# Pooling attention and a residual MLP on one core: the first batch recorded in parts by a written list, token weights in two transfers

## The chip, the cores and the metric

One core of a Trainium2 chip. The metric is the device time of one execution in microseconds (us). The kernel has five compute engines: TensorE (PE) for matmuls and transposes, VectorE (DVE), ScalarE (ACT), GpSimd (POOL), and SyncE (SP), which here only issues transfers. Transfers are also issued by POOL (all those that change the number format on the way) and a few by ACT.

## The reference

Eight batches, eight heads, 576 positions, head width 64. Keys and values are averaged over groups of eight positions, so that each query sees 72 of them; the attention output, heads side by side, is the input x of a residual MLP of width 512.

```python
k_p = k.reshape(B, H, Sp, pool, D).mean(axis=3)
v_p = v.reshape(B, H, Sp, pool, D).mean(axis=3)
scores = scale * np.matmul(q, k_p.transpose(0, 1, 3, 2))
scores = scores - np.max(scores, axis=-1, keepdims=True)
attn = np.exp(scores)
attn = attn / (np.sum(attn, axis=-1, keepdims=True) + 1e-09)
x = np.matmul(attn, v_p)        # heads then side by side: (8, 576, 512)

a1 = alpha1 * x + beta1
tok = np.einsum('ts,bsd->btd', w_tok, a1)
u = x + lam * tok
a2 = alpha2 * u + beta2
ch = np.maximum(a2 @ w_ch1, 0.0) @ w_ch2
out = u + lam * ch
```

## The kernel before

Positions are handled in chunks of 128: four whole chunks per batch, and the last 64 positions of two batches together as a fifth. Four chunks make a block of 512 tokens for the MLP; there are nine. Work is recorded in a fixed order and each engine runs its own instructions in that order, one after another; waits between engines go over semaphores. From the second batch on, the order comes from a list of due times per block (the loop over `n` near the end): while the MLP of one block runs, the attention of the next batch is strewn in. The first batch has no MLP to hide under. Its order, from `load_w1(0)` to the last `mlp_A(0, j, 256, 512)`, is written out by hand, and this opening is what is changed.

The parts of the opening, with their lines in the kernel before:

- Loads. q, k, v of batch 0, the token weights (`load_wtok`, L387 for the four main rows per partition and L391 for the last 64 rows), the first part of w_ch1 (`load_w1(0)`, L560), then q (L267) and k (L281) of batch 1 are all issued by POOL, ahead of its own arithmetic. The other parts of w_ch1, v of batch 1 and w_ch2 (`load_w1`, `load_v32`, `load_w2`) are issued by POOL further on, between its other work.
- Attention of batch 0. `att_F` transposes q for two heads on PE (L594) and copies it out of PSUM; `att_Frem` does so for the last 64 positions. `double_k` and `cast_rem_k` prepare k on DVE; `att_K` averages k with matmuls (L671, L677); `first_V` does the same for v (L698, L700). `att_S` is the scores of one head in two halves (L719, L722), each followed by its exponential on ACT (L724). `att_AV` multiplies by v (L783, L787); DVE takes the reciprocal of the sum and scales (L789, L791).
- Input of the token product. `spread_lamal` spreads lambda times alpha1 over all partitions with a matmul (L503) and a copy. `att_X` multiplies two heads of x by it into `xs` (L805), `rest_X` does so for the last positions (L798); in the opening most of these run on POOL. `bias_row` writes the beta1 row of `xs` on DVE (L478).
- Token weights. `setup_wtok` transposes 128 rows of the token weights on PE (L521) and ACT copies them to `wtT` (L524). `setup_rowsum` sums the columns with matmuls (L533) and ACT copies one row (L535). `setup_vectors` turns beta2 and alpha2 into columns (L508 to L512).
- Token product and first layer. `mix_T` multiplies a chunk's `wtT` by `xs` (L869, five matmuls of 512 columns), DVE adds x (L873), and DVE or POOL multiplies by alpha2 (L879). `mix_uT` transposes the result (L893), ACT copies it to `u_fm` (L895). `mlp_A` is the first MLP layer (L917): in block 0 the hidden parts 0 to 3 are done for the first 256 tokens and then for the second 256, with the bias column taken on DVE (L920) and the ReLU on ACT (L924).

PSUM has eight banks. Six belong to the pool `psA`, from which `gp` hands out one bank after another in turn; two belong to `psB`, which the opening before uses only for the warm-up matmuls (`keep_warm`, L860). A new tile in a bank waits until the last reader of the old one is done.

Before the change a part is a function that records its matmuls and the copy out of PSUM at once, so that a later part's matmul comes behind the earlier part's copy in the list, though on another engine:

```python
setup_wtok(0, nc.scalar.copy)
att_AV(0, 6)
load_rem(1, behind=nc.vector)
setup_wtok(1, nc.scalar.copy)
```

Of the kernel before, what the change touches and what calls it, by code (L numbers as in the profile page):

```python
# [210 lines left out]
def kernel(  # L211
# [27 lines left out]

    def gp(name):  # L240
        return psA.tile([P, 512], FP, tag="gp", name=name)

# [256 lines left out]
    def spread_lamal(half, copy):  # L499

        ps = gp("ps_bc")[:, 0:256]
        cols = slice(256 * half, 256 * half + 256)
        nc.tensor.matmul(out=ps, lhsT=ones_row, rhs=vecs[0:1, 2, cols])  # L503
        copy(out=lamal_bc[:, cols], in_=ps)

    def setup_vectors():
        ps = gp("ps_vec")
        nc.tensor.transpose(out=ps[:, 0:8], in_=b2row, identity=identity[0:8, 0:8])  # L508
        nc.scalar.copy(out=b2c_bf, in_=ps[:, 0:4])
        nc.scalar.copy(out=al2_cols, in_=ps[:, 4:8])  # L510
        u_fm[0] = work.tile([P, 4, 2, 258], BF, tag="u_fm", bufs=3, name="u_fm")
        nc.scalar.copy(out=u_fm[0][:, :, 0, 256], in_=ps[:, 0:4])  # L512

    def setup_wtok(tcx, copy):

        trc = P if tcx < 4 else REM
        w = wt_bf[0:trc, S * tcx:S * tcx + 640]
        strided = w[:, 0:512].rearrange("p (m c) -> p c m", c=4)
        ps_w = gp("ps_w").bitcast(BF)
        for sc in range(5):  # L520
            nc.tensor.transpose(out=ps_w[0:P, trc * sc:trc * sc + trc],  # L521
                                in_=strided[:, sc, :] if sc < 4 else w[:, 512:640],
                                identity=identity_bf[0:trc, 0:trc])
        copy(out=wtT[:, 0:5, P * tcx:P * tcx + trc],  # L524
             in_=ps_w[:, 0:5 * trc].rearrange("p (s t) -> p s t", t=trc))

    def setup_rowsum(tcx):

        trc = P if tcx < 4 else REM
        cols = slice(P * tcx, P * tcx + trc)  # L530
        ps = gp("ps_rs")
        for sc in range(5):
            nc.tensor.matmul(out=ps[:, 0:trc], lhsT=ones_bf if sc < 4 else ones_lo,  # L533
                             rhs=wtT[:, sc, cols], start=(sc == 0), stop=(sc == 4))
        nc.scalar.copy(out=wtT[64:65, 4, cols], in_=ps[64:65, 0:trc])  # L535
# [44 lines left out]
    def att_F(b, hp, copy=nc.scalar.copy):  # L580
# [4 lines left out]
        if r == 0:  # L585
# [14 lines left out]
        def finish(copy):  # L600
            copy(out=st["qT"][u][:, 4 * r:4 * r + 4, :],
                 in_=ps_q[:, 0:512].rearrange("p (c t) -> p c t", c=4))

        if copy is None:
            return finish
        finish(copy)

    def att_Frem(b, copy=None):
# [14 lines left out]
        for c in range(2):  # L623
            nc.tensor.transpose(out=ps_q[:, 128 * c:128 * c + 128],
                                in_=st["rem"][0][:, c].rearrange("p h d -> p (h d)"),
                                identity=identity_bf)
        copy(out=st["rem_qT"], in_=ps_q[:, 0:256].rearrange("p (c t) -> p c t", c=2))

    def double_k(u):

        nc.vector.tensor_copy(out=st1[0]["k"][u][:, :, 4], in_=st1[0]["k"][u][:, :, 0])
        if u == 0:
            cast_rem_k(nc.vector)
# [29 lines left out]
    def att_K(b, u, copy):  # L663
# [18 lines left out]
        if b:  # L682
            copy(out=kp_pool[u], in_=kp)
            return
        for a in range(2):
            rows = slice(64 * a, 64 * a + 64)
            (copy or (nc.scalar.copy, nc.vector.tensor_copy)[a])(
                out=kpT_pool[u][rows, a], in_=kp[rows])

    def first_V(b, u, copy=nc.vector.tensor_copy):  # L690
# [8 lines left out]
        for c in range(nr):  # L699
            nc.tensor.matmul(out=vp, lhsT=pool_vr if b else pool_vr[0:32],  # L700
                             rhs=rest[:, heads, c], start=False,
                             stop=(c == nr - 1))
        copy(out=vp1_pool[u][:, :, 0:64], in_=vp.rearrange("p (h d) -> p h d", h=4))
# [8 lines left out]
    def att_S(b, h):  # L712
        st = st1[b]
        u, r, hh = h // 4, h // 2 % 2, h % 2
        ET = ET_pool[u][:, h % 4]
        for half in range(2):
            n0, n = 256 * half, 256 + 64 * half
            ps_sc = gp("ps_sc")
            nc.tensor.matmul(out=ps_sc[0:SPG, 0:256], lhsT=kpT_pool[u][:, half, h % 4, :],  # L719
                             rhs=st["qT"][u][:, 2 * (h % 4):2 * (h % 4) + 2, :])  # L720
            if half:
                nc.tensor.matmul(out=ps_sc[0:SPG, 256:320], lhsT=kpT_pool[u][:, hh, h % 4, :],  # L722
                                 rhs=st["rem_qT"][:, :, h // 2::4].rearrange("p c i -> p i c"))
            nc.scalar.activation(out=ET[:, n0:n0 + n], in_=ps_sc[0:SPG, 0:n],  # L724
                                 func=AF.Exp, bias=0.0, scale=0.125)
# [47 lines left out]
    def att_AV(b, h):  # L773
# [13 lines left out]
        nc.tensor.matmul(out=av[:, 4 - 4 * odd, :], lhsT=ET[:, r0:r0 + 128], rhs=vp1[:, h % 4, :])  # L787
        rec = recs[:, h, b, :]
# [53 lines left out]
    u_fm = {}  # L842
# [19 lines left out]
    def mix_T(b, c, eng=nc.vector):  # L862
# [3 lines left out]
        for sc in range(5):  # L866
            for i, p0, p1 in parts:
                kk, at = (P, sc) if sc < 4 else (P, 5) if i else (65, 4)
                nc.tensor.matmul(out=ps_tok[p0:p1], lhsT=wtT[0:kk, at, P * c:P * c + p1 - p0],  # L869
                                 rhs=xs_pool[i][0:kk, sc, :], start=(sc == 0), stop=(sc == 4))  # L870
        for i, p0, p1 in parts:
# [3 lines left out]
                                    in1=ps_tok[p0:p1, 0:DM], op=ALU.add)  # L875
        if b:
# [4 lines left out]
    def mix_uT(key):  # L881
# [10 lines left out]
        for cc in range(4):  # L892
            nc.tensor.transpose(out=ps_uT[0:P, 128 * cc:128 * cc + 128],  # L893
                                in_=s["u_bf"][:, 128 * cc:128 * cc + 128], identity=identity_bf)
        nc.scalar.copy(out=u_fm[blk][:, :, at // 2, 128 * (at % 2):128 * (at % 2) + 128],  # L895
# [10 lines left out]
    def mlp_A(n, j, t0=0, t1=512):  # L906
# [5 lines left out]
        for cc in range(4):  # L912
            if n == 0:
                rhs = u_fm[0][:, cc, 0, 0:257] if one else u_fm[0][:, cc, t0 // 256:2, 0:256]
            else:
                rhs = u_fm[n][:, cc, :]
            nc.tensor.matmul(out=ps_h[:, t0:t1 + one], lhsT=w1_of(cc, j), rhs=rhs,  # L917
                             start=(cc == 0), stop=(cc == 3))
        if one:
# [138 lines left out]
    for u in range(2):  # L1058
        load_k(1, u, queue=nc.gpsimd)
    keep_warm(16)  # L1060
    att_F(0, 0)
    second_copy = att_F(0, 1, None)
    cast_rem(0, nc.vector)
    more_constants()
    rem_copy = []
    att_Frem(0, lambda **io: rem_copy.append(io))
    double_k(0)
    second_copy(nc.vector.tensor_copy)
    att_K(0, 0, None)
    nc.scalar.copy(**rem_copy[0])  # L1070
    first_V(0, 0)
    bias_row(0)
    att_S(0, 0)
    att_S(0, 1)
    double_k(1)
    att_S(0, 2)
    att_AV(0, 0)
    spread_lamal(0, nc.vector.tensor_copy)
    att_AV(0, 1)
    att_S(0, 3)  # L1080
    att_K(0, 1, nc.scalar.copy)
    att_F(0, 2, nc.vector.tensor_copy)
    att_AV(0, 2)
    late_copy = att_F(0, 3, None)
    att_X(0, 0, 2, nc.gpsimd, False)
    spread_lamal(1, nc.scalar.copy)
    att_S(0, 4)
    late_copy(nc.scalar.copy)
    att_AV(0, 3)
    att_X(0, 2, 4, nc.gpsimd, False)  # L1090
    first_V(0, 1)
    att_S(0, 5)
    load_al2(nc.vector)
    att_AV(0, 4)
    att_S(0, 6)
    rest_X(0, 0, 4, nc.gpsimd)
    att_AV(0, 5)
    att_X(0, 4, 6, nc.gpsimd, False)
    att_S(0, 7)
    setup_wtok(0, nc.scalar.copy)  # L1100
    att_AV(0, 6)
    load_rem(1, behind=nc.vector)
    setup_wtok(1, nc.scalar.copy)
    att_AV(0, 7)
    setup_rowsum(0)
    setup_wtok(2, nc.scalar.copy)
    rest_X(0, 4, 6, nc.gpsimd)
    load_w1(1)
    setup_wtok(3, nc.scalar.copy)
    setup_rowsum(1)  # L1110
    setup_vectors()
    setup_wtok(4, nc.scalar.copy)
    att_X(0, 6, 8)
    bias_row(1)
    mix_T(0, 0, nc.gpsimd)
    setup_rowsum(2)
    load_w1(2)
    mix_T(0, 1)
    setup_rowsum(3)
    load_lam(nc.vector)  # L1120
    mix_T(0, 2, nc.gpsimd)
    load_v32(1)
    mix_uT((0, 0))
    mix_uT((0, 1))
    mix_T(0, 3)
    load_w2(0)
    load_w2(1)
    mlp_A(0, 0, 0, 256)
    mix_uT((0, 2))
    mlp_A(0, 1, 0, 256)  # L1130
    mlp_A(0, 2, 0, 256)
    mix_uT((0, 3))
    mlp_A(0, 3, 0, 256)
    for j in range(4):
        mlp_A(0, j, 256, 512)


    def attention(b):
# [4 lines left out]
        if first:  # L1143
            for hp in range(4):
                todo.append((2.6 + 0.9 * hp, lambda hp=hp: att_F(b, hp)))
# [3 lines left out]
            todo.append((7.4, lambda: att_Frem(b, nc.scalar.copy)))  # L1149
        if b < B - 1:  # L1150
            at = 28.5 if first else 10.0
            todo.append((at, lambda: att_F(b + 1, 0)))
            todo.append((at + 0.1, lambda: att_F(b + 1, 2)))
            todo.append((19.3 if first else 23.1, lambda: cast_rem(
                b + 1, nc.gpsimd, behind=None if first else nc.vector)))
            todo.append((26.72 if b > 1 else 26.22, lambda: att_Frem(b + 1)))
        for u in range(2):
# [8 lines left out]
            if first:  # L1166
                todo.append((19.1 + 0.1 * u, lambda u=u: sum_k(2, u, nc.gpsimd)))
            todo.append((7.0 + 2.3 * u if first else 2.9 + 2.0 * u,
                         lambda u=u: att_K(b, u, nc.vector.tensor_copy if first else nc.scalar.copy)))
        for u in range(2):  # L1170
# [5 lines left out]
            for i, dt in enumerate((2.9, 3.4, 4.6, 5.1) if u else early):  # L1176
                h = 4 * u + i
                todo.append((at + dt, lambda h=h: att_AV(b, h)))
# [3 lines left out]
        if first:  # L1182
            for i, u in enumerate((0, 2, 1)):
                todo.append((10.6 + 0.1 * i, lambda u=u: sum_v(b, u)))
            for u in range(2):
                todo.append((12.3 + 1.0 * u, lambda u=u: first_V(b, u)))
# [3 lines left out]
        for c in range(5):  # L1190
            at = 22.0 + 1.1 * c if first else 21.0 + (1.3 if b == 2 else 1.15) * c
            if c < 4 or b % 2:
                todo.append((at, lambda c=c: mix_T(b, c)))
                key = (b, c) if c < 4 else (b - 1, 4)
                todo.append((at + 1.8, lambda key=key: mix_uT(key)))
        return todo

    for n in range(NBLK):
        todo = []
        for j in range(0 if n else 4, NJ):  # L1200
            if n == 0 and j < 8:
                todo.append((j, lambda j=j: mlp_A(0, j, 0, 256)))
                todo.append((j + (1.01 if j < 7 else 0.3), lambda j=j: mlp_A(0, j, 256, 512)))
            else:
                at = 8 * (j // 4 % 2) + 4 * (j // 8) + j % 4 if n >= FIRST else j
                todo.append((at, lambda j=j: mlp_A(n, j)))
# [51 lines left out]
        if n == 0:  # L1258
            todo.append((6.2, lambda: setup_rowsum(4)))
# [58 lines left out]
```

## Time and profile before

| | |
|---|---|
| Median of 3 runs | 331.59 us (330.57 to 332.87) |
| Profiled execution | 331.99 us, of which the span is 330.5 us |
| PE busy | 320.9 us (97%) |
| DVE busy | 235.0 us (71%) |
| ACT busy | 174.5 us (53%) |
| POOL busy | 117.8 us (36%) |
| Moved by transfers | 47.72 MB, 144 GB/s over the span |

The span is the time from the first to the last instruction that the profile shows; the profiled execution's own time is 1.5 us longer. Shares are over the whole span and hide that stages have different limits. A row of the timeline gives start, duration, engine, line, operation, what is written from what, how many instructions of the kind follow each other, and in brackets the idle time ahead of it with what ended it. Where several matmuls are in one row, the duration runs to the end of the last one, which is pipelined, so that the start of the next row tells better how long they kept PE. For a transfer, the duration of the instruction is only the issue; its landing is given apart.

### The profile page before, as it was taken

The page shows a single profiled execution, that of the slowest core. Times are in us where ns is not written, and L with a number is a line of the kernel's source. Part 1 is how long each engine was busy: PE and PEld are TensorE (multiplying, and loading weights), DVE is VectorE, ACT ScalarE, POOL GpSimd, SP SyncE. Part 2 cuts the span into 40 slices and gives each one's busy share as a digit, 9 for nine tenths or more (in the row PEclk, how much of TensorE's full clock was granted, in tenths as well). Part 3 has the DMA queues.
Part 4 walks back from the last instruction along what each step waited for, and adds up shares of the span by engine and source line. Part 5 has one row for each costly group of instructions (what it writes and reads, how often), then busy time and mean ns, then how long its engine had stood idle before and what let it go on. Part 6 is the DMA issues. An engine that isn't in the chain of part 4 may idle for free.

```text
span 330.5 us, 6433 instructions
## 1 busy us (share of the span) xinstructions
PE 320.9 (97%) x2436; PEld 206.6 (63%) x2467; DVE 235.0 (71%) x495; ACT 174.5 (53%) x323; POOL 117.8 (36%) x142
## 2 busy tenths in 40 slices
PE   8989999999999999999999999999999999999995
PEld 3657764445544567656775676558755866586584
DVE  6764276897769979787869787877788793263263
ACT  1675989459522871288028812682268225703710
POOL 8859625997238001800271026202520560000000
PEclk9999999999999999999999999999999999999999
DMA  7999999957897993399439953998560025003013
GB/s 105 191 219 293 277 180 234 182 134 186 167 258 107 194 178 126 82 242 195 156 80 216 214 161 77 173 202 154 144 170 9 2 51 160 0 2 127 0 34 95
DMA packets 73370, 47.72 MB, mean 144 GB/s; under 512 B 41165, under 2 KB 63829, under 8 KB 73338
## 3 DMA queue, kind: packets, MB, share of 16 engines
q1 hardware_dynamic: 58876, 34.50, 44.8%
q0 software_dynamic: 13856, 12.40, 22.4%
q10 hardware_dynamic: 606, 0.40, 0.5%
q8 instruction: 19, 0.31, 0.4%
q14 instruction: 13, 0.11, 0.1%
HBM read 38.57 MB, written 9.44 MB: 145 GB/s over the span
## 4 chain that ended last, share of the span: by engine, by line
PE 89%; DMA 3%; DVE 3%; POOL 2%; issue 1%; ACT 0%; POOLq 0%
PE ps_h L917 38%; PE ps_w L1033 26%; PE ps_tok L869 11%; PE ps_ch L937 7%; DMA wt_bf<-in_moe_w_tok_dram 3%; PE ps_s L739 2%; PE ps_av L783 2%; DVE w L968 1%; DVE u_sb L873 1%; PE ps_r L746 1%; PE ps_av L787 1%; POOL v L301 0%; POOL k L273 0%; ACT wtT L524 0%; POOL u_bf L879 0%
## 5 line engine op out<-in xcount | busy, mean ns | idle before, releaser
L917 PE MATMUL ps_h<-u_fm,w 128*128 128x512 bf16 (+2 forms) x588 | 131.3, 368 | 1.7 <-DVE u_sb L947 0.6
L924 ACT ACTIVATE H<-ps_h,bias_cols 128x512 bf16<-128x512 f32 x144 | 98.1, 688 | 55.4 <-PE ps_h L917 54.0
L917 PEld LDWEIGHTS <-w 128*128 128x128 bf16 x608 | 65.9, 114 | 51.4 <-issue 3.3
L1033 PEld LDWEIGHTS <-H 128*128 128x128 bf16 x560 | 53.5, 98 | 10.8 <-DVE u_sb L1051 1.2
L877 ACT CAST u_bf<-u_sb 128x512 bf16<-128x512 f32 x32 | 19.8, 618 | 70.7 <-issue 41.8
L1033 PE MATMUL ps_w<-w,H 128*128 128x256 bf16 x448 | 53.6, 273 | 0.0
L805 POOL TENSOR_TENSOR xs<-x_tm,lamal_bc 128x512 bf16<-128x512 f32 x12 | 15.2, 1268 | 105.0 <-DVE x_tm L791 104.5
L1051 DVE TENSOR_TENSOR u_sb<-u_sb,ps_w 128x512 f32<-128x512 f32 x54 | 36.4, 684 | 17.9 <-PE ps_w L1033 17.0
L869 PE MATMUL ps_tok<-xs,wtT 128*128 128x512 bf16 (+2 forms) x193 | 44.5, 380 | 0.7 <-DVE xs L805 0.3
L873 DVE TENSOR_TENSOR u_sb<-x_tm,ps_tok 128x512 f32<-128x512 f32 (+1 forms) x40 | 27.4, 684 | 9.8 <-PE ps_tok L869 9.8
L791 DVE TENSOR_TENSOR x_tm<-ps_av,recs 128x320 f32<-128x320 f32 x64 | 31.5, 491 | 2.7
L768 ACT ACTIVATE ET<-ps_s 72x512 f16<-72x512 f32 x56 | 32.3, 592 | 0.0
L937 PE MATMUL ps_ch<-w,H 128*128 128x512 bf16 x124 | 30.0, 379 | 0.2
L869 PEld LDWEIGHTS <-wtT 128*128 128x128 bf16 (+3 forms) x200 | 17.4, 100 | 16.4 <-issue 1.1
L789 DVE RECIPROCAL recs<-ps_av 128x5 f32<-128x5 f32 x64 | 12.1, 189 | 19.0 <-PE ps_av L787 18.8
L709 DVE TENSOR_TENSOR v_u<-v_u 72x1024 f32<-72x1024 f32 (+1 forms) x24 | 23.6, 985 | 0.2
L1033 PE MATMUL ps_w<-w_t,h_s 128*128 128x256 bf16 x168 | 22.6, 272 | 0.0
L937 PEld LDWEIGHTS <-H 128*128 128x128 bf16 x128 | 11.9, 98 | 13.7 <-issue 0.4
L378 POOL TENSOR_TENSOR k_raw<-k_raw 128x512 f32<-128x512 f32 x14 | 19.1, 1367 | 3.5 <-DMA k_raw<-in_k_dram 3.5
L380 POOL TENSOR_TENSOR k_bf<-k_raw 128x512 bf16<-128x512 f32 x14 | 19.2, 1370 | 1.1
L1002 DVE TENSOR_TENSOR h_s<-H 128x1024 bf16<-128x1024 bf16 x21 | 14.6, 696 | 6.3 <-ACT H L924 5.8
L1033 PEld LDWEIGHTS <-h_s 128*128 128x128 bf16 x168 | 16.4, 98 | 4.1
(165 smaller groups left out, 358.1 us busy)
## 6 DMA issues: line engine op xcount, KB each, us to landing
out_dram<-u_sb SPq DMA_DIRECT2D x29, 256.0 KB, 4.3
k_raw<-in_k_dram SPq DMA_DIRECT2D x12, 512.0 KB, 6.0
v_u<-in_v_dram SPq DMA_DIRECT2D x12, 512.0 KB
q_bf<-in_q_dram POOLq DMA_DIRECT2D x16, 256.0 KB, 6.1
w<-in_moe_w_ch_dram POOLq DMA_DIRECT2D x6, 512.0 KB, 13.3
out_dram<-u_sb SPq DMA_DIRECT2D x11, 128.0 KB, 2.2
w<-in_moe_w_ch_dram POOLq DMA_DIRECT2D x1, 1024.0 KB, 14.5
k_raw<-in_k_dram POOLq DMA_DIRECT2D x2, 512.0 KB, 16.8
```

Source lines behind the costliest of these rows:

```text
L380: eng.tensor_tensor(out=bf, in0=twice[0], in1=twice[1], op=ALU.add)
L709: nc.vector.tensor_tensor(out=out, in0=t[:, :, 0:width], in1=t[:, :, width:2 * width], op=ALU.add)
L768: nc.scalar.activation(out=o, in_=i, func=AF.Exp, bias=0.0, scale=0.125 if b < 3 else 0.125 * 0.125)
L791: nc.vector.tensor_tensor(out=x[:, 1 - odd:6 - odd, dd:dd + D], in0=av[:, :, 0:64], in1=rec.unsqueeze(2).to_broadcast((P, 5, D)), op=ALU.mult)
L869: nc.tensor.matmul(out=ps_tok[p0:p1], lhsT=wtT[0:kk, at, P * c:P * c + p1 - p0], rhs=xs_pool[i][0:kk, sc, :], start=(sc == 0), stop=(sc == 4))
L873: nc.vector.tensor_tensor(out=s["u"][p0:p1, :], in0=x[p0:p1, 1 + c if c < 4 else 5 - 5 * i, :], in1=ps_tok[p0:p1, 0:DM], op=ALU.add)
L877: nc.scalar.copy(out=s["u_bf"], in_=s["u"])
L917: nc.tensor.matmul(out=ps_h[:, t0:t1 + one], lhsT=w1_of(cc, j), rhs=rhs, start=(cc == 0), stop=(cc == 3))
L924: nc.scalar.activation(out=H4[n, j // 4][:, j % 4, :], in_=ps_h, func=AF.Relu, bias=bias_cols[:, j:j + 1], scale=1.0)
L937: nc.tensor.matmul(out=ps, lhsT=H_of(n, j)[:, 128 * m:128 * m + 128], rhs=w2[j // 4][:, j % 4, :], start=(j == 0), stop=(j == NJ - 1))
L1033: nc.tensor.matmul(out=ps, lhsT=stat(j), rhs=moving(j), stop=(j == 7), start=(first and (pp == 0 or alone) and j == 0), skip_group_check=True)
L1051: nc.vector.tensor_tensor(out=o, in0=o, in1=banks[key, "both"], op=ALU.add)
```

## The change

The opening is recorded in parts. The functions become generators: the matmuls of a part are recorded up to a `yield`, the copy or the arithmetic on the result at the next call. A dictionary `plan` holds one generator under a short name for each part, and a written list of names, `order`, says which of them is taken one step further. For the rest of the kernel `whole` runs a generator to its end at once, which records the same as before.

With it come these edits:

- `load_wtok` issues the four main rows in two transfers of 1216 and 1088 columns instead of one of 2304. The first serves W0 and W1, the second W2 and (with the short transfer) W3.
- `spread_lamal` (s0, s1) stands ahead of k on PE.
- Seventeen of the opening's PSUM tiles, named in `in_pair`, come from `psB` instead of `psA`, so that eight banks turn instead of six.
- The heads are done in another order (2, 3, 1, 0, 5, 4, 7, 6 or near to it, halves apart), some copies change their engine, and the `xs` pieces (X and R) change their order.
- The k loads of batch 1 (k0, k1) go from ahead of the opening to between the parts; the second and third part of w_ch1 (l1, l2) go ahead of k0 and k1. v of batch 1 (lv) and two parts of w_ch2 (l3, l4) stand between the token products.

In the names, F, K, V, S, A, X, R, W, r, M, T, H and G stand for `att_F`, `att_K`, `first_V`, the scores, `att_AV`, `att_X`, `rest_X`, `setup_wtok`, `setup_rowsum`, `mix_T`, `mix_uT`, and the two halves of `mlp_A`.

```diff
+    pair = [False]
+
     def gp(name):
+        if pair[0]:
+            return psB.tile([P, 512], FP, tag="ch", bufs=2, name=name)
         return psA.tile([P, 512], FP, tag="gp", name=name)
+
+    def whole(parts):
+        for _ in parts:
+            pass
...
     def load_wtok():
-        nc.gpsimd.dma_start(out=wt_bf[:, 0:4 * S],
-                            in_=moe_w_tok[0:512, :].rearrange("(p c) s -> p (c s)", c=4))
+        main = moe_w_tok[0:512, :].rearrange("(p c) s -> p (c s)", c=4)
+        for c0, c1 in ((0, 2 * S + 64), (2 * S + 64, 4 * S)):
+            nc.gpsimd.dma_start(out=wt_bf[:, c0:c1], in_=main[:, c0:c1])
...
         nc.tensor.matmul(out=ps, lhsT=ones_row, rhs=vecs[0:1, 2, cols])
+        yield
         copy(out=lamal_bc[:, cols], in_=ps)
...
     load_q_bf(1, 0)
     load_q_bf(1, 1)
-    for u in range(2):
-        load_k(1, u, queue=nc.gpsimd)
     keep_warm(16)
...
+    plan = {"dr": once(lambda: cast_rem_k(nc.vector)), "b0": once(lambda: bias_row(0)),
+            "b1": once(lambda: bias_row(1)), "Fr": att_Frem(0, vector),
+            "ve": setup_vectors(), "la": once(lambda: load_al2(nc.vector)),
+            "lr": once(lambda: load_rem(1, behind=nc.vector)),
+            "ll": once(lambda: load_lam(nc.vector)), "lv": once(lambda: load_v32(1)),
+            "l1": once(lambda: load_w1(1)), "l2": once(lambda: load_w1(2)),
+            "l3": once(lambda: load_w2(0)), "l4": once(lambda: load_w2(1))}
+    for u in range(2):
+        plan[f"d{u}"] = once(lambda u=u: double_k(u))
+        plan[f"k{u}"] = once(lambda u=u: load_k(1, u, queue=nc.gpsimd))
+    for u, copies in enumerate(((scalar, scalar), (vector, vector))):
+        plan[f"K{u}"] = att_K(0, u, *copies)
...
+    for h, n, eng in ((0, 4, nc.gpsimd), (2, 0, nc.gpsimd), (4, 2, nc.gpsimd), (6, 2, nc.vector)):
+        plan[f"X{h}"] = once(lambda h=h, eng=eng: att_X(0, h, h + 2, eng, False))
+        plan[f"R{h}"] = once(lambda h=h, n=n, eng=eng: rest_X(0, h, h + n, eng))
...
+    for c, eng in enumerate((nc.vector, nc.gpsimd, nc.vector, nc.gpsimd)):
+        plan[f"r{c}"] = setup_rowsum(c)
+        plan[f"M{c}"], plan[f"T{c}"] = mix_T(0, c, eng), mix_uT((0, c))
+        plan[f"H{c}"], plan[f"G{c}"] = mlp_A(0, c, 0, 256), mlp_A(0, c, 256, 512)
+    in_pair = "A2 A6 F1 Fr H2 H3 M1 M3 S2a S3b S4b S5a S7a T0 W2 W3 r2".split()
+    order = (
+        "dr d0 b0 F1 F0 s1 F1 s0 K0 l1 Fr s1 K0 s0 V0 K0 Fr F0 S2a S2b S3b d1 V0 S1b S1a K1 k0 "
+        "K1 S2a S0a S2b K1 S1b S3a S0b A2 F2 F2 S1a S3b S3a S0a F3 A2 A3 A3 l2 k1 S4a S0b S5b "
+        "F3 S5b S5a S5a A1 S4a V1 la S4b A0 V1 S4b S7a S7b S6a A1 A5 A0 S6a S7b A5 A4 S6b W1 "
+        "X2 S7a S6b R0 W0 W0 W1 A7 ve A4 A7 lr A6 X0 X4 W4 W3 R4 lv W3 A6 ve r0 r1 W2 X6 r1 R6 "
+        "r3 r0 M1 W2 b1 M1 M0 W4 r2 r3 M0 r2 M1 l3 l4 M3 T1 T1 M0 ll T0 M2 T0 H0 M3 H1 M2 M3 "
+        "M2 T3 T2 H2 H1 H0 T3 H3 T2 H2 G0 G0 G2 H3 G2 G3 G3 G1 G1")
+    for name in order.split():
+        pair[0] = name in in_pair
+        next(plan[name], None)
+    pair[0] = False
```

More of the change, by code (lines that the diff above doesn't have):

```diff
@@ L598, in att_F @@
                 identity=identity_bf)
[L600 to L606, printed above, removed]
+        yield
+        copy(out=st["qT"][u][:, 4 * r:4 * r + 4, :],
+             in_=ps_q[:, 0:512].rearrange("p (c t) -> p c t", c=4))
     def att_Frem(b, copy=None):
@@ L661, in pool_k, with att_K @@
             in_=rest_sums[:, :, 2 * u:2 * u + 2])
-    def att_K(b, u, copy):
+    def att_K(b, u, *copies):
         st = st1[b]
@@ L682, in att_K @@
         if b:
-            copy(out=kp_pool[u], in_=kp)
+            copies[0](out=kp_pool[u], in_=kp)
             return
-        for a in range(2):
+        for a, copy in enumerate(copies):
+            yield
             rows = slice(64 * a, 64 * a + 64)
-            (copy or (nc.scalar.copy, nc.vector.tensor_copy)[a])(
-                out=kpT_pool[u][rows, a], in_=kp[rows])
+            copy(out=kpT_pool[u][rows, a], in_=kp[rows])
     def first_V(b, u, copy=nc.vector.tensor_copy):
@@ L710, in att_V, with scores @@
                                 op=ALU.add)
-    def att_S(b, h):
-        st = st1[b]
-        u, r, hh = h // 4, h // 2 % 2, h % 2
+    def scores(h, half):
+        st = st1[0]
+        u, hh = h // 4, h % 2
         ET = ET_pool[u][:, h % 4]
[L716 to L725, printed above, removed]
+        n0, n = 256 * half, 256 + 64 * half
+        ps_sc = gp("ps_sc")
+        nc.tensor.matmul(out=ps_sc[0:SPG, 0:256], lhsT=kpT_pool[u][:, half, h % 4, :],
+                         rhs=st["qT"][u][:, 2 * (h % 4):2 * (h % 4) + 2, :])
+        if half:
+            nc.tensor.matmul(out=ps_sc[0:SPG, 256:320], lhsT=kpT_pool[u][:, hh, h % 4, :],
+                             rhs=st["rem_qT"][:, :, h // 2::4].rearrange("p c i -> p i c"))
+        yield
+        nc.scalar.activation(out=ET[:, n0:n0 + n], in_=ps_sc[0:SPG, 0:n],
+                             func=AF.Exp, bias=0.0, scale=0.125)
         st["ET"][h] = ET
@@ L841 @@
     u_of = {}
-    u_fm = {}
+    u_fm = {0: work.tile([P, 4, 2, 258], BF, tag="u_fm", bufs=3, name="u_fm")}
     def chunk_of(b, c):
@@ L1097 @@
[L1097 to L1135, printed above, removed]
+    def once(do):
+        do()
+        yield
+    vector, scalar = nc.vector.tensor_copy, nc.scalar.copy
```

89 lines of the change are left out of this document (37 added, 52 removed).

## The prediction

> **What bounds the kernel now.** I read the page first, then the chain of waits, then the timelines of TensorE (PE) and GpSimd (POOL) over the first 45 us, then the table of DMA issues. The chain, in order of time:
>
> ```profile
> 8.73 10.19 DMA wt_bf<-in_moe_w_tok_dram
> 18.96 0.48 PE ps_w L521 x5
> ...
> 21.49 0.70 DVE xs L805
> ...
> 22.24 0.39 PE ps_tok L869
> ...
> 27.04 1.28 POOL u_bf L879
> ...
> 30.54 1.92 PE ps_h L917 x16
> ```
>
> The reader sees the opening: the token weights land at 18.92, then transposes, the last part of xs, the first token product (M0) at 22.24, two more element-wise steps, and at 30.54 the last work of the opening (G, 1.92 us). PE reaches batch 1 at 32.30 (first row of L594 after 30). From there it is PE that sets the time, as the windows show, but for 7 us in which VectorE does:
>
> ```profile
> 30.50:61.90 31.40, 31.26 (x274) 19.88 (x276) 17.15 (x46) 27.98 (x51) 18.42 (x20) 1.00 1.04 231
> 61.90:69.00 7.10, 6.48 (x34) 2.55 (x32) 6.91 (x9) 1.24 (x2) 7.02 (x7) 1.00 0.73 110
> 69.00:330.00 261.00, 256.45 (x1879) 167.18 (x1906) 190.34 (x372) 129.29 (x229) 69.17 (x82) 1.00 0.59 129
> ```
>
> (PE, weight load, DVE, ACT, POOL busy, clock, DMA share, GB/s.) The diff leaves that code alone, so the question is when PE gets to 32.30. POOL in the opening:
>
> ```profile
> 12.58 0.76 POOL L281 DMA_DIRECT2D k_raw<-in_k_dram  x1 [0.48 <-DVE k L631]
> 14.36 0.76 POOL L281 DMA_DIRECT2D k_raw<-in_k_dram  x1 [1.02 <-PE ps_kp L677]
> 15.13 1.28 POOL L805 TENSOR_TENSOR xs<-x_tm,lamal_bc 128x512 bf16<-128x512 f32 x1
> 16.80 1.26 POOL L805 TENSOR_TENSOR xs<-x_tm,lamal_bc 128x512 bf16<-128x512 f32 x1 [0.39 <-DVE x_tm L791]
> 18.02 0.71 POOL L798 TENSOR_TENSOR xs<-x_tm,lamal_bc 64x256 bf16<-64x256 f32 x1
> 19.11 1.28 POOL L805 TENSOR_TENSOR xs<-x_tm,lamal_bc 128x512 bf16<-128x512 f32 x1 [0.37 <-ACT ET L724]
> 20.34 0.46 POOL L798 TENSOR_TENSOR xs<-x_tm,lamal_bc 64x128 bf16<-64x128 f32 x1
> ```
>
> Its five xs pieces (X and R in the plan) fill the time while the token weights are on their way, 15.13 to 20.80. And the queue that POOL issues into, with us from issue to landing:
>
> ```profile
> q_bf<-in_q_dram POOLq DMA_DIRECT2D x4, 256.0 KB, 11.1
> w<-in_moe_w_ch_dram POOLq DMA_DIRECT2D x1, 1024.0 KB, 14.5
> k_raw<-in_k_dram POOLq DMA_DIRECT2D x2, 512.0 KB, 16.8
> wt_bf<-in_moe_w_tok_dram POOLq DMA_DIRECT2D x1, 576.0 KB, 10.2
> ```
>
> Up to 16.8 us of backlog, served in order of issue. Landings, each from its issue plus its own time: last v piece 15.0, wt_bf 18.92 and its short rest 19.07, w1 24.3, the two q of batch 1 26.4 and 28.1, the two k 29.5 and 31.1.
>
> **The change, part by part.** What decides is in the built program. Transfers from POOL take eight completion semaphores in turn, and each waits until the one eight places earlier has landed. One transfer more (wt_bf in two), and two w1 pieces moved ahead of the k loads, put the second k load of batch 1 (k1) at place 17: it waits for place 9, the second half of wt_bf. Before, k1 waited for a q that lands at 13.7. In POOL's list all five xs pieces stand behind k1 now. The loads of v and w2 (lv, l3, l4) are moved up likewise: l4 waits for the second q (28.1), and the multiply that ends token block 3 (M3, POOL) stands behind it.
>
> - Second half of wt_bf lands: the bytes ahead of it are the same, so 18.92 is the upper end. Of wt_bf's sixteen completion counts fifteen came by 17.72, and the last at 18.91, after a 16 KB instruction packet had held an engine for 0.96 us at 16.89. That packet should come some 0.4 us earlier, as PE stands further on in its list. Ends 17.7 and 18.9; I take 18.7, since the packet still falls among these bytes.
> - k1: 0.2 to 0.5 from release to issue in the two L281 rows, plus 0.76: xs starts at 19.7.
> - xs on POOL, by start-to-start times of the rows: 1.23 + 0.68 + 1.23, and 1.28 for the last X: 24.1. R4 (0.46) is needed only for the fifth matmul. First token product (M1) at **24.2**, against 22.24.
> - From M1 on, PE: M1 and M0 2 x 1.09 (23.61 to 24.70 in the timeline), row sum 0.28, M3 1.09, eight transposes 0.54, M2 1.09: 29.4; H0, H1 0.88, T3 0.22: 30.5. T2 waits: M2 ends 29.55, add 0.69 and multiply 0.69 on DVE: 31.0. T2 0.22, H2 and H3 0.88: 32.1, just when ACT has copied T2 (0.59). G 4 x 0.44: batch 1 at **33.9**, against 32.30: **+1.6 us**.
> - The second gate: l4 released at 28.1, issue 0.2 + 0.57, M3's multiply 1.28: T3 not before 30.2. T3, T2 and their copies (0.59 and 0.50 on ACT) give G at 31.8 at the earliest, +1.2 even if the first gate were open. It hides behind the first now.
> - wt_bf's first half should land near 16.3, but PE is only at W1 near 17.1. W1 and W0 start 1.9 earlier than L521 did; M1 waits for xs, so this is worth nothing on the path. W4, W3, W2 and four row sums end by 21.4: cover 2.8 us. If the halves landed together at 18.9, W1 and W0 (0.44) would stand ahead of A7 and A6 on PE; two pairs of reciprocal and scale (0.65 each) and X6, R6 on DVE end near 22: still covered.
> - Spread of lambda*alpha1 ahead of k: two matmuls of 0.31 at 8.4 instead of 12.3 and 14.7. k16's doubling moves behind the two casts and the bias row (0.68) ahead of F1's copy on DVE; K0 loses some 0.3 us, its copies go to ACT alone (0.37 more). All ends before POOL is free: 0.
> - Eight banks, heads reordered: 16 exps on ACT still take 0.3 each; attention ends near 19.5 on DVE. Nothing is left on the path: 0.
> - Loads behind the opening: k0 lands after q (28.1), w1 piece (2.5, the spacing of the w1 pieces) and its own 1.4: 32.0; two sums of 1.28 on POOL: 34.7, needed at 35.98 + 1.6. k1 at 36.2, sums 38.9, needed at 40.23 + 1.6. Cover 2.9 each; it would be gone if the opening became 1.3 us shorter.
>
> Sum: profiled execution 331.99 (span 330.5 and 1.5 around it) + 1.6 = 333.6; it lies 0.40 above the median of the runs shown, 331.59, so **333.2**.
>
> **The clock.** No row of before has PE idle for longer than 0.64 us; here it idles from 21.4 to 24.2. What a slow array costs is in the warm-up: its first 13 matmuls of 512 columns start 427 ns apart, later ones 216, the change coming 5.8 us after the first (the granted clock reads 1.00 there too, so it doesn't tell). If the idle time brought that back, up to 5.8 us from M1 run at half rate: 2.9 lost at most, 2.0 where the 0.5 before T2 absorbs some; nothing if it doesn't.
> The Trainium skill ("TensorE: Matmul & The Clock Gate", Part 1 on the HAM clock gate) puts the fall to half clock after one idle window of about 3.4 us, and its table of goals warns of idle gaps beyond about 3 us. By the first figure 2.8 us of idleness stays at full clock and the sum is 333.2, by the second it is at the edge; no run here shows it yet.
>
> **Rivals.**
> 1. The array falls to half rate in the gap (above): 333.2 + 2.0 to 2.9, so about 335.6. For it: a gap four times the longest seen, after a stretch of short transposes. Against: it is no longer than half of the 5.8 us that the rise took.
> 2. Not slower: the gates don't hold, because the second half lands with the first (near 16.5) and the q loads before 26. Then xs would be done near 21.5, M1 near 21.8, and 7.9 to G gives 29.7 or, with M3's multiply, 29.9: 0.6 gained, 331.0. It decides if k1 is issued before 16.8. Against: landings follow order and bytes in every row above, and more than 1.3 us can't be gained, as k1's sums show.
> 3. The split doesn't do what it says (halves land together): the covers above hold, 333.2 again, so it is part of the forecast.
> 4. Only the second gate counts (second half at 17.7): +1.2, 332.8; inside the forecast's range.
>
> **How the numbers follow.** Forecast with 3 and 4: 0.70, own range 332.3 to 334.0. Rival 1: 0.22. Rival 2: 0.06. Something later, such as a landing near 20: 0.02. Range 331.8 to 335.9: it leaves out rival 2 and the tails. The bound of 1% (about what a measurement of this kernel can tell from no change) is 3.3 us: the forecast and rival 2 lie within it, most of rival 1 beyond 334.9. Faster 0.02, same 0.73, slower 0.25.
>
> **What would show it.** On POOL no xs row before 18.5, and a wait of the second k load that ends with wt_bf; five xs pieces in a row to about 24.5; PE idle 2 to 3 us before the first ps_tok, at about 24.2; a w2 issue that waits until about 28; the 256-column half of ps_h at about 32.1 and batch 1's ps_q at 33.9. M1's matmuls 216 ns apart mean the clock held, 427 rival 1. An xs row on POOL before 17 would make the forecast wrong, and so would a shift at 33.9 that is gone by 62.

## The result, and the profile after

| | before | after |
|---|---|---|
| Median of 6 runs | 331.51 us | 336.1 us (334.62 to 336.45) |
| Profiled execution | 331.99 us, span 330.5 | 336.31 us, span 334.8 |
| First ps_q of batch 1 on PE | 32.30 | 36.63 |

The ratio of after to before is 1.0129, with an interval of 1.0101 to 1.0157: slower by 1.0 to 1.6%. (Where a few executions of a kernel were disturbed, its ratio here and below leaves them out.)

The span is 4.3 us longer, and PE comes to batch 1 4.33 us later. So the place to look is the opening. The stages behind it, cut 4.3 us later than in the prediction's windows, show the same work on PE at the same pace; in the first of them POOL and the transfers are a little less busy than before (columns: PE, weight load, DVE, ACT, POOL busy, clock, DMA share, GB/s):

```profile
34.83:66.20 31.37, 31.37 (x278) 19.88 (x277) 17.36 (x46) 27.95 (x51) 15.62 (x16) 1.00 0.86 200
66.20:73.30 7.10, 6.56 (x35) 2.57 (x33) 6.87 (x9) 1.24 (x2) 7.02 (x7) 1.00 0.77 109
73.30:334.30 261.00, 257.88 (x1906) 167.17 (x1906) 190.24 (x372) 129.34 (x229) 69.22 (x82) 1.00 0.59 129
```

The chain of waits, in order of time:

```profile
20.21 0.50 DVE x_tm L801
20.76 0.05 issue
20.81 3.99 DVE xs L815
24.80 0.05 issue
24.84 3.82 PE ps_tok L879 x10
...
31.68 0.70 DVE u_sb L884
32.41 1.30 DVE u_bf L891
33.71 0.05 issue
33.76 0.40 PE ps_uT L905 x4
34.15 2.64 PE ps_h L930 x24
```

Three pieces are too long. X6 on DVE took 0.70 before and takes 3.99. The ten matmuls of M1 and M0 take 3.82 and not 2.3. M2's multiply (u_bf) takes 1.30 and not 0.70. POOL's timeline over the same time:

```profile
17.47 0.74 POOL L572 DMA_DIRECT2D w<-in_moe_w_ch_dram  x1 [0.40 <-DMA wt_bf<-in_moe_w_tok_dram]
19.05 0.75 POOL L289 DMA_DIRECT2D k_raw<-in_k_dram  x1 [0.83 <-DVE recs L799]
19.82 1.30 POOL L815 TENSOR_TENSOR xs<-x_tm,lamal_bc 128x512 bf16<-128x512 f32 x1
21.06 0.74 POOL L808 TENSOR_TENSOR xs<-x_tm,lamal_bc 64x256 bf16<-64x256 f32 x1
21.75 2.48 POOL L815 TENSOR_TENSOR xs<-x_tm,lamal_bc 128x512 bf16<-128x512 f32 x2
24.18 0.91 POOL L808 TENSOR_TENSOR xs<-x_tm,lamal_bc 64x128 bf16<-64x128 f32 x1
...
30.83 1.28 POOL L891 TENSOR_TENSOR u_bf<-u_sb,al_bc 128x512 bf16<-128x512 f32 x1 [0.51 <-DVE u_sb L884]
32.06 0.39 POOL L371 CAST rem_q<-rem_raw 128x256 bf16<-128x256 f32 x1
32.43 0.71 POOL L374 TENSOR_TENSOR rem_k<-rem_raw 128x256 bf16<-128x256 f32 x1
```

The two load issues at 17.47 (l2) and 19.05 (k1) stand ahead of all five xs pieces. The trace's landing records put the two halves of wt_bf at 17.19 and 18.46, so the issues come 0.28 and 0.58 us behind the landing eight places earlier. (The profile names DVE's reciprocal for the second wait; but in after, e3, e4, e5 and e8 alike k1 is issued 0.58 to 0.59 us behind that landing.) This wait of k1 is called the gate below. The xs pieces, which ran from 15.13 to 20.80 before, run from 19.82 to 25.09. The issues, with us to landing, show the same backlog as before and the two parts of the token weights:

```profile
q_bf<-in_q_dram POOLq DMA_DIRECT2D x4, 256.0 KB, 11.0
w<-in_moe_w_ch_dram POOLq DMA_DIRECT2D x1, 1024.0 KB, 14.3
k_raw<-in_k_dram POOLq DMA_DIRECT2D x2, 512.0 KB, 17.0
...
wt_bf<-in_moe_w_tok_dram POOLq DMA_DIRECT2D x1, 304.0 KB, 8.5
wt_bf<-in_moe_w_tok_dram POOLq DMA_DIRECT2D x1, 272.0 KB, 9.2
```

The matmuls of M1 and M0 are long because of the clock. Three windows of 3.41 us, columns as above:

```profile
21.05:24.47 3.42, 0.72 (x10) 0.54 (x9) 3.42 (x1) 1.97 (x9) 3.42 (x5) 1.00 1.23 219
24.47:27.88 3.41, 3.04 (x8) 1.11 (x9) 2.06 (x4) 0.00 (x0) 2.13 (x3) 0.50 1.31 212
27.88:31.29 3.41, 3.41 (x27) 1.90 (x26) 2.02 (x5) 1.26 (x3) 2.82 (x4) 1.00 1.17 281
```

PE idled 2.96 us ahead of M1, busy for 0.72 us of the first window; in the second the granted clock is 0.50 throughout, and then 1.00 again.

### The profile page after: what moved, and what is told of

It reads as the page before. It is cut to its first block, busy times and chain, and to the rows that moved or that the text cites. A ratio compares the mean times of both kernels' runs of the same rounds, so it can differ in the third digit from the quotient of the medians.

```text
span 334.8 us, 6462 instructions
## 1 busy us (share of the span) xinstructions
PE 323.6 (97%) x2467; PEld 207.2 (62%) x2467; DVE 239.4 (72%) x496; ACT 174.1 (52%) x322; POOL 119.1 (36%) x143
## 4 chain that ended last, share of the span: by engine, by line
PE 90%; DVE 5%; DMA 2%; POOL 1%; issue 1%; POOLq 0%; DVEq 0%
PE ps_h L930 37%; PE ps_w L1047 26%; PE ps_tok L879 12%; PE ps_ch L951 7%; PE ps_s L748 2%; PE ps_av L792 2%; DMA k<-in_k_dram 2%; DVE xs L815 1%; DVE w L982 1%; DVE x_tm L801 1%; DVE u_sb L884 1%; PE ps_r L755 1%; PE ps_av L796 1%; PE ps_kp L678 0%; DVE u_bf L891 0%
## 5 line engine op out<-in xcount | busy, mean ns | idle before, releaser
L930 PE MATMUL ps_h<-u_fm,w 128*128 128x512 bf16 (+2 forms) x608 | 132.7, 368 | 0.6 <-DVE u_sb L961 0.6
L879 PE MATMUL ps_tok<-xs,wtT 128*128 128x512 bf16 (+3 forms) x200 | 46.2, 389 | 3.0 <-DVE xs L815 3.0
L777 ACT ACTIVATE ET<-ps_s 72x512 f16<-72x512 f32 x56 | 32.3, 591 | 0.0
L1016 DVE TENSOR_TENSOR H<-H,H 128x1024 bf16<-128x1024 bf16 x14 | 9.6, 689 | 13.5 <-ACT H L938 13.4
```

The source lines that it names most:

```text
L777: nc.scalar.activation(out=o, in_=i, func=AF.Exp, bias=0.0, scale=0.125 if b < 3 else 0.125 * 0.125)
L1016: nc.vector.tensor_tensor(out=o, in0=a, in1=b, op=op)
```

## The experiments

Labels e1 to e13 are names only. In the table, M1 is the start of the first token product on PE and ps_q the first transpose of batch 1; the last column is the ratio to the kernel before, with its interval.

| kernel | M1 | ps_q | median us | ratio |
|---|---|---|---|---|
| before | 22.24 (M0) | 32.30 | 331.51 | 1 |
| after | 24.84 | 36.63 | 336.1 | 1.0129 (1.0101 to 1.0157) |
| e5 before, with the new load order | 25.07 (M0) | 37.55 | 336.24 | 1.0123 (1.0074 to 1.0173) |
| e1 after, k1 later | 22.39 | 35.75 | 334.42 | 1.007 (1.0028 to 1.0112) |
| e3 after, with filler matmuls | 24.72 | 35.08 | 334.32 | 1.0088 (1.006 to 1.0116) |
| e8 e3, with l3 and l4 later | 25.04 | 34.86 | 333.69 | 1.0053 (1.0027 to 1.0079) |
| e4 after, one token transfer | 24.59 | 35.88 | 336.82 | 1.0157 (1.0113 to 1.0202) |
| e9 after, with the old load order | 21.06 | 30.87 | 330.91 | 0.9985 (0.9968 to 1.0001) |
| e12 e9, six banks | 21.32 | 31.13 | 330.89 | 0.9965 (0.9934 to 0.9996) |
| e11 e9, one token transfer | 22.44, see below | 32.25 | 331.93 | 0.9997 (0.9975 to 1.0019) |
| e13 the same again | 21.83 | 31.63 | 332.27 | 1.002 (1.0 to 1.004) |
| e7 after, all waits behind the arithmetic | 20.93 | 30.74 | 332.23 | 1.001 (0.9983 to 1.0037) |
| e10 e7, k0 ahead of l1 | 21.37 | 31.18 | 331.95 | 0.9999 (0.9979 to 1.002) |

**e5: the load order alone.** In the kernel before, the parts of w_ch1 and the k loads of batch 1 are put ahead of POOL's xs; nothing else changes.

```diff
     load_q_bf(1, 1)
-    for u in range(2):
-        load_k(1, u, queue=nc.gpsimd)
     keep_warm(16)
...
     att_K(0, 0, None)
+    load_w1(1)
     nc.scalar.copy(**rem_copy[0])
...
     att_K(0, 1, nc.scalar.copy)
+    load_k(1, 0, queue=nc.gpsimd)
+    load_w1(2)
+    load_k(1, 1, queue=nc.gpsimd)
     att_F(0, 2, nc.vector.tensor_copy)
...
     rest_X(0, 4, 6, nc.gpsimd)
-    load_w1(1)
...
     setup_rowsum(2)
-    load_w1(2)
```

> The kernel before with only the loads reordered as in the change: second part of w_ch1, k0, third part of w_ch1, k1, all ahead of POOL's first xs piece; heads, banks, order of PE and the one transfer of the token weights as before. Theory (POOL's queue): k1 waits for the token weights (18.9), xs starts at 19.7 instead of 15.1, the first token product at 24.5 to 25 instead of 22.24: 2.3 to 2.8 later, and 1.5 more if PE's idle stretch of about 3 us halves its clock; time 334.0 to 335.8. Rival (order of heads, banks): unchanged, 331.5.

336.24 us: 0.4 above the upper end, and as slow as the whole change. POOL and PE:

```profile
19.28 0.75 POOL L281 DMA_DIRECT2D k_raw<-in_k_dram  x1 [4.04 <-PE ps_w L521]
20.05 2.52 POOL L805 TENSOR_TENSOR xs<-x_tm,lamal_bc 128x512 bf16<-128x512 f32 x2
```

```profile
25.07 2.32 PE L869 MATMUL ps_tok<-xs,wtT 128*128 128x512 bf16 x5 [3.37 <-DVE xs L805]
```

The k load waits for the (undivided) token weights, xs starts at 20.05 behind it, PE idles for 3.37 us, and the first five token matmuls take 2.32 us instead of 1.25. The clock stays at half for twice 3.41 us here. So the order of the loads is enough for the loss; banks, heads and the split are not needed for it.

**e9: everything but the load order.** The new opening with the loads where the kernel before has them:

```diff
-        ... K0 l1 Fr ... S1a K1 k0 K1 ... A3 A3 l2 k1 S4a ... W3 R4 lv W3 ... r2 M1 l3 l4 M3 ... M2 M3 M2 ...
+        ... K0 Fr ... S1a K1 K1 ... A3 A3 S4a ... W3 R4 l1 W3 ... r2 M1 l2 M3 ... M2 M3 lv l3 l4 M2 ...
```

and `load_k(1, u)` again ahead of `keep_warm(16)`.

> The change without its order of loads: heads, banks, spread, split token weights and the list as in the new kernel, but the loads where the kernel before has them (k0 and k1 ahead of the opening, l1 behind R4, l2 behind M1's multiply, lv, l3 and l4 behind M3's multiply). My theory: nothing of the loss remains, M1 near 21.9, ps_q of batch 1 at 31.6 to 32.3, 330.5 to 331.3 if the kernel before reads 331.2. Rival (the other parts of the change cost too): ps_q after 32.5, 331.8 or more.

330.91 us, as expected; PE comes to batch 1 at 30.87, 1.43 ahead of the kernel before and earlier than the 31.6 to 32.3 that I gave. POOL's xs:

```profile
15.20 0.76 POOL L289 DMA_DIRECT2D k_raw<-in_k_dram  x1 [0.57 <-PE ps_av L796]
15.97 1.28 POOL L815 TENSOR_TENSOR xs<-x_tm,lamal_bc 128x512 bf16<-128x512 f32 x1
17.25 0.74 POOL L808 TENSOR_TENSOR xs<-x_tm,lamal_bc 64x256 bf16<-64x256 f32 x1
17.95 2.51 POOL L815 TENSOR_TENSOR xs<-x_tm,lamal_bc 128x512 bf16<-128x512 f32 x2
```

The xs pieces start 3.85 us earlier than after (15.97 and 19.82), and M1 comes 3.78 earlier (21.06 and 24.84). With e5 this shows from both sides that the loss comes from where the loads stand. It shows too that the rest of the change makes a shorter opening, which the load order hid.

**e3 and e8: what happens behind M1.** e3 puts twelve warm-up matmuls (2.75 us) on PE in the idle time ahead of M1:

```diff
+            "kw": once(lambda: keep_warm(12)),
...
-        "r3 r0 M1 W2 b1 M1 M0 ...
+        "r3 r0 kw M1 W2 b1 M1 M0 ...
```

> The changed kernel with 12 matmuls on zeros (as in the warm-up) put into PE's idle stretch ahead of the first token product; nothing else. Theory (PE fell to half rate because it idled, and that costs 1.5 us of the ten matmuls behind the gap): the granted clock is 1.00 throughout, M1's and M0's matmuls start 216 ns apart, batch 1's first ps_q comes at 35.1 instead of 36.6, time 334.6. Rival (the slow stretch is swallowed by the later wait for M2's and M3's multiplies): clock full but time 336.1 as before.

334.32 us, as the theory had it. M1 stays (24.72), the clock is 1.00 throughout, and its ten matmuls take 2.33 us:

```profile
24.72 2.33 PE L879 MATMUL ps_tok<-xs,wtT 128*128 128x512 bf16 x10 [1.25 <-DVE xs L815]
```

From M1 to ps_q it is 10.36 us, against 11.79 after: the half clock costs 1.43 in the opening. What stays above the 9.7 of my sum is on DVE. e8 is e3 with the two w2 loads moved behind M3's multiply:

```diff
-        "... r2 M1 l3 l4 M3 ... M2 M3 M2 ...
+        "... r2 M1 M3 ... M2 M3 l3 l4 M2 ...
```

> The new kernel with the 12 filler matmuls of the earlier run (e3), and l3 and l4 moved behind M3's multiply. In e3, M2's multiply on VectorE took 1.25 us, ending 0.55 after the end of POOL's rem_k sum, and ps_q of batch 1 came at 35.08. If it is POOL's arithmetic on SBUF that holds VectorE's multiply, POOL issues transfers at that time now, the multiply takes 0.69, and ps_q comes 0.5 to 0.6 earlier, at 34.5: 333.7 where e3 had 334.3. Rival (the multiply is slow for another reason, such as transfers writing to SBUF): 1.2 us again, 334.3.

333.69 us, as the theory had it. M2's multiply on DVE, first in e3, then in e8:

```profile
30.88 1.25 DVE L891 TENSOR_TENSOR u_bf<-u_sb,al_bc 128x512 bf16<-128x512 f32 x1
```

```profile
31.21 0.72 DVE L891 TENSOR_TENSOR u_bf<-u_sb,al_bc 128x512 bf16<-128x512 f32 x1
```

In e3 POOL casts rem_q and sums rem_k meanwhile; in e8 it issues transfers from 30.82 to 31.96. M1 to ps_q is 9.82 now, 0.54 less. ps_q itself came at 34.86 and not at 34.5, as M1 was 0.32 later in this execution.

**e1: one wait taken away.** k1 is issued behind POOL's last xs piece (R4):

```diff
-        ... A3 A3 l2 k1 S4a ... W3 R4 lv W3 ...
+        ... A3 A3 l2 S4a ... W3 R4 k1 lv W3 ...
```

> The changed kernel with one name of the order moved: the second k load of batch 1 (k1) stands behind POOL's last xs piece instead of ahead of its first. Theory (POOL's queue: k1 waits for the second half of the token weights, and the xs pieces wait behind it): xs starts at 18.2 instead of 19.8, the last xs piece of DVE ends near 23.3, the first token product starts at 23.4 instead of 24.8, PE idles only some 1.5 us before it and keeps its full clock; M3's multiply still stands behind the w2 load that waits for q (28.3), so batch 1's first ps_q comes near 33.4 instead of 36.6. Time about 332.7. Rival (the new order of heads and the eight banks make DVE or ACT late, POOL's queue costs nothing): no change, 336.1.

334.42 us: less than after, but 1.7 above what I expected. M1 came at 22.39 at full clock, 1.0 earlier than I had it, as xs started at 17.36 and not at 18.2. Batch 1 came at 35.75 all the same, and not at 33.4. What POOL did behind M1's start:

```profile
23.40 0.90 POOL L317 DMA_DIRECT2D v_main<-in_v_dram  x1
26.23 0.60 POOL L319 DMA_DIRECT2D v_rest<-in_v_dram  x1 [1.94 <-PE ps_tok L879]
26.84 1.27 POOL L891 TENSOR_TENSOR u_bf<-u_sb,al_bc 128x512 bf16<-128x512 f32 x1
28.09 0.60 POOL L578 DMA_DIRECT2D w<-in_moe_w_ch_dram  x1
29.41 0.53 POOL L578 DMA_DIRECT2D w<-in_moe_w_ch_dram  x1 [0.73 <-DMA q_bf<-in_q_dram]
29.96 1.28 POOL L891 TENSOR_TENSOR u_bf<-u_sb,al_bc 128x512 bf16<-128x512 f32 x1
```

The short transfer of v (v_rest) is place 19 and waits for place 11, the first part of w_ch1, which lands near 25.7 here. M1's multiply, ready at 24.37 when its addition on DVE was done, starts at 26.84 behind it, and M3's multiply at 29.96 behind l4's wait. So the new order has three waits in a row, and in after the first hid the other two. M2's multiply on DVE, beside POOL's arithmetic, took 2.18 here (30.64 to 32.82), and PE waited 1.18 for it.

**e4: the split undone in the new kernel.** One transfer of 2304 columns:

> The changed kernel with the token weights' main rows in one transfer again. k1 then waits for that one transfer, which lands no later than the second half. Theory (the split is worth nothing, as the first token product waits for xs): W1 and W0 start near 18.7 instead of 18.3, the first token product and the time as in the changed kernel, 335.8 to 336.4. Rival (the earlier first half pays): slower by 0.5 or more, 336.6 and up. A third outcome, faster, would mean that the extra transfer itself costs.

336.82 us. The median is on the rival's side, but the interval overlaps that of after, and neither M1 (24.59 and 24.84) nor ps_q (35.88 and 36.63) is later. k1, now at place 16, waits for the whole of wt_bf, and xs starts at 19.57. In the opening the split shows no worth behind that wait; the times leave open whether it has some.

**e7 and e10: the new loads, with no arithmetic behind a wait.** In e7 l2 and k1 go behind R4, and lv, l3 and l4 behind M3's multiply.

> The new opening, but every load of POOL that has to wait for an earlier landing stands where that landing is past or where no arithmetic is behind it: l2 and k1 behind R4, and v and the two w2 parts (lv, l3, l4) behind M3's multiply. My theory (the whole loss is POOL's waits for landings, and what follows from them: X6 held by POOL's run, the half clock, M2's multiply held): POOL's xs start near 16.2, its last whole piece ends near 20.9, M1 at 21.8, no matmul at half rate, M2's multiply 0.69 us, batch 1's first ps_q at 31.5 to 31.9 against 32.30 before; that is 330.4 to 331.1 if the kernel before reads 331.2. Rival A (the heads' order, the banks or the split cost something of their own): M1 later than 22.3 or ps_q later than 32.4, 331.6 or more. Rival B (the later loads starve batch 1): ps_q as above, but PE idle between 36 and 45 us, 332 or more.

The opening is the shortest of all (30.74), yet the time is 332.23. Rival B's wait is there:

```profile
35.36 0.29 PE L678 MATMUL ps_kp<-pool_main,k_bf 128*128 128x64 bf16 x4 [0.77 <-POOL k_bf L388]
```

PE waits for the sums of batch 1's first k, which lands behind a part of w_ch1. How much of the 1.3 us between the medians of e7 and e9 is this wait stays open. In e10 that k (k0) changes places with l1:

> The kernel of e7 with k0 ahead of l1, so that the first k of batch 1 lands one w1 piece (2.5 us) earlier. In e7 PE waited 0.77 us for k0's sums on POOL at 34.6 to 35.4. If that is why e7 read 332.2 where e9 read 330.9: no such wait, ps_q at 30.7 to 30.9 as in e7 and e9, 330.9 to 331.3. Rival (the late l2 and k1, still behind R4, cost something themselves): 332 again, with PE idle elsewhere before 50 us.

331.95 us: outside what the theory gave. The wait for k0 is gone, but PE now waits 0.34 us at 39.5 for the second k, still late, and 0.32 us at 110.2 for an averaged k in the scores of batch 3. In the waits of PE behind 20 us:

```profile
PE ps_kp L678 <- POOL k_bf L388: 0.3, 1, 0.3
PE ps_s L748 <- DVE kp L666: 0.3, 1, 0.3
```

e12 below has neither, and a span 0.6 shorter with nearly the same ps_q (329.7 and 330.3). But only the first of the two belongs to the late loads: e11 and e13 below have the old loads, and PE waits 0.32 and 0.33 us for the averaged k there too. So a later k1 costs 0.34 us of PE in this trace, and the rival is shown no further. From ps_q to the end of the span the profiled executions take 297.7 us in e9, 298.2 before, 298.6 in e12, 298.7 in e13, 298.9 in e7, 299.1 in e10 and 299.4 in e11. The kernels with the old loads alone differ by 1.6 us there, so a difference of a few tenths in the opening can't be read from these times.

**e12, e11 and e13: what makes the short opening.** e12 is e9 with an empty `in_pair`, so that all tiles come from six banks.

> The kernel of e9 (the change with the loads where the kernel before has them), with all PSUM tiles of the opening from the six banks again. My prediction gave the two more banks nothing. In e9 M1 starts at 21.06 with the row sums of PE right ahead of it and no wait for a bank in sight, so: M1 at 21.1, ps_q at 30.9, the time of e9 (0.998 of the kernel before). Rival (the banks are what makes this opening shorter): M1 at 22 or later, ps_q near 32, no faster than before.

330.89 us, 0.9965 of before: the same as e9, and the only kernel here whose whole interval lies below 1. ps_q is 0.26 later than in e9, but xs started 0.29 later too (16.26), behind a k load that waited for a landing 0.29 later. The two more banks bring nothing that these runs show. e11 is e9 with one transfer for the token weights:

> The kernel of e9 (the change without its order of loads) with the token weights in one transfer again. My prediction gave the split nothing, because xs was the later one; in e9 xs is early and M1 starts at 21.06 right behind the row sums. In the run with one transfer and the new loads (e4), the last row sum of the same four ended at 21.7, so M1 comes at 21.7 to 21.8 here, ps_q at 31.5, 331.5 where e9 had 330.9. Rival (the split is worth nothing here either): M1 at 21.1, 330.9.

331.93 us (ratio 0.9997, 0.9975 to 1.0019). Its profiled execution ran at half clock from 11.65 to 15.07, so its M1 (22.44) can't be laid to the split. The same kernel once more is e13:

> The kernel of e11 (the loads of the kernel before, the token weights in one transfer) once more, since the opening of e11's profiled execution ran in part at half clock, from about 12 to 15 us, so that its M1 at 22.44 does not count. As for e11: M1 at 21.7 to 21.8 and ps_q at 31.5 if the split is worth 0.6 to 0.7 us in an opening that does not wait for loads, the same as e9 (21.06 and 30.87) if it is worth nothing.

332.27 us, M1 at 21.83, ps_q at 31.63: 0.5 to 0.8 later than e12 and e9. The transposes W1 and W0 on PE, first in e9, then in e13:

```profile
17.29 0.76 PE L531 MATMUL ps_w<-identity_bf,wt_bf 128*128 128x128 bf16 x10
```

```profile
18.50 0.75 PE L531 MATMUL ps_w<-identity_bf,wt_bf 128*128 128x128 bf16 x10 [1.15 <-DMA wt_bf<-in_moe_w_tok_dram]
```

With one transfer PE waits 1.15 us for its landing (18.45), and between there and M1 the profile shows no more than 0.22 us of waiting. So in these traces the split is worth half a microsecond or more in an opening that does not wait for loads. The times bear it out only in part: the interval of e13 (1.0 to 1.004) lies above that of e12, but that of e11, the same kernel, overlaps both e12's and e9's. Against before, e13's ps_q is 0.67 earlier (31.63 and 32.30). Of this, 0.41 is M1, and the token weights happened to land 0.46 earlier in this execution (18.45 and 18.91); so only the 0.26 from M1 on (9.80 and 10.06) is left for the list, that is for the heads, the parts and the order of the xs pieces, which no run told apart. e13's time shows nothing of it.

## Why the prediction was right or wrong

**The gate: right.** k1 waits for the second half of wt_bf and holds POOL's xs. I had xs at 19.7 and X4's end at 24.1; they are 19.82 and 24.23.

**M1 at 24.2: 0.64 too early.** It starts at 24.84. The step let X4 on POOL release it; in fact X6 on DVE did, which I took for covered ("X6, R6 on DVE end near 22"). X6 began at 20.81 and lasted 3.98 us. In five traces it ended 0.54 to 0.56 us behind POOL's X4: 24.23 and 24.79 after, 21.78 and 22.33 in e1, 24.02 and 24.57 in e3, 24.45 and 25.01 in e5, 20.46 and 21.00 in e9. Where it started only once X4 was done, it took its normal time:

```profile
20.91 0.69 DVE L815 TENSOR_TENSOR xs<-x_tm,lamal_bc 128x512 bf16<-128x512 f32 x1
```

(DVE's timeline in e13, where POOL's X4 ended at 20.48.) X6 does not wait for a semaphore of POOL; it was held while POOL ran.

**From M1 to batch 1, 9.7: right where nothing disturbs it** (9.81 in e9, 9.82 in e8), but 11.79 after. e3 and e8 give the difference: 1.43 for the half clock, 0.54 for M2's multiply. From e9 to after the shift is 5.76 = 3.78 (M1) + 1.43 + 0.54 + 0.01; from before to after it is 4.33 = 5.76 - 1.43, where the last is what the rest of the change gains (it equals the half clock's price by chance). Against the forecast, ps_q is 2.73 late (36.63 and 33.9): 0.64 is M1, 1.43 the half clock, 0.54 M2's multiply, and 0.1 the sum's own error.

**The clock: the likeliest case was the wrong one.** This is the step of the forecast that failed: it gave the idle gap ahead of M1 no price, and the half clock cost 1.43. Rival 1, at 0.22, is what happened, on top of the forecast's own gate. Its 335.6 is near 336.1, which lies 0.2 above the upper end of the range (335.9, on that end, by the ratio on the forecast's 331.59). That it is so near is partly luck: its price for the clock was too high, and what it lacked (0.64 for X6, 0.54 for M2's multiply) made up for that. My argument against it, that the gap was no longer than half of the 5.8 us in which the clock had risen at the start, compared the wrong things: in these traces the clock changes in fixed windows of 3.41 us, and a gap of 2.96 nearly emptied one. The trace of before has no record of the clock ahead of 7.52 us, so the 1.00 that I read in the warm-up was no measurement. I had the price at 2.0 to 2.9; e3 has 1.43 in the opening and 1.8 between the medians (1.4 between the ratios). One window at half rate can cost 1.7 at most, half of 3.41, and in the profiled execution only one was lost; e5 lost two. The mean clock of two other executions of after is 0.989 and not 0.995, as for two lost windows, yet they took 336.0 and 336.2; so what a second one costs stays open.
The Trainium skill ("TensorE: Matmul & The Clock Gate", Part 1 on the HAM clock gate) gives a free-running window of 3413 ns, and the clock records of after show half clock for 3413 ns. Its figure of one idle window before the fall is not what decided: the window before the fall had 0.72 us of matmuls in it.

**The second gate: its place was right, its price not.** Behind the first gate it cost no wait of its own, as I wrote. But with the first gate open I gave +1.2 (rival 4), and e1 has +3.45 at ps_q. I had named l4 and M3, and left out the short v transfer, which in e1 held M1's multiply from 24.37 to 26.84, and M2's multiply on DVE, which took 2.18.

**Edits costed at nothing.** Eight banks: right (e12). The split: nothing to be seen in the opening behind the gate (e4), but 0.5 to 0.8 without it (e13). Heads and list: no more than 0.26 is shown (e13), where I had nothing. The k loads: covered after, and the cover was gone where I said; with the opening 1.56 shorter (e7) PE waited 0.77 for k0.

**Rival 2** (not slower) fell with its condition: k1 was not issued before 16.8.

## What to carry to other kernels

A load that is issued by an engine which also computes is an instruction in that engine's order, and its wait for an older landing holds all arithmetic behind it (3.8 us of M1 here). When loads are moved ahead, list for each the landing that it must wait for and the work that stands behind it, for every load and not only for the first that binds; opening one such wait only uncovers the next. A stall of PE of some 3 us had a second price in the clock here, and elementwise work on DVE and POOL was not independent where both read all their inputs from SBUF.

## What the runs showed of the hardware

**DVE held by POOL.** A DVE multiply with both inputs in SBUF (X6, 0.69 us alone) took 1.0 to 5.0 us while POOL did multiplies on SBUF without a pause, and ended 0.54 to 0.56 us behind X4; up to four POOL instructions were done in that time (e3: from 19.58 to 24.57). DVE's addition that reads PSUM (u_sb<-x_tm,ps_tok) kept its 0.69 us beside a POOL multiply: in e1 it ran from 29.91, POOL's multiply from 29.96 for 1.28. The converse exists too: R4, which stands right behind X4 on POOL, took 0.91 instead of 0.46 in after.
The Trainium skill ("SBUF — State Buffer", section "Who interferes with whom" and the one on its two sides) describes a port pair that GpSimd and VectorE share as an exclusive lock, for a DVE instruction with two SBUF inputs against a GpSimd instruction that reads SBUF; the traces agree that one waits for the other. By the page the one that starts first holds it for a whole instruction. The runs do not settle who comes next: in e3 X6's record starts at 19.58, ahead of POOL's first xs piece at 19.61, and four of POOL's instructions still went ahead of it; but R4 behind them did not, there as in after.

**Half clock in blocks.** The granted clock fell to 0.50 for 3.41 us (after, e4, e11) or 6.827 us (e5). PE had been busy for 0.72 us (after), 1.13 (e4), 1.71 (e5) and 2.40 (e11, short matmuls alone) of the 3.41 us before. In e1 windows with 1.92 and 1.71 us busy were followed by full clock. So no limit in busy time divides the cases; what does stays open.
